# Retention and a soft mixture of experts on one core: input and weight loads of 8 KB per partition, and a separate ring of eight small tiles

## The chip, the cores and the metric

The kernel runs on one core of a Trainium2 chip. The metric is the device time of one execution in microseconds (us). The kernel before takes 169.75 us (median of three runs, 169.55 to 169.78).

## The reference

The reference computes a decayed linear attention (a "retention") over 4 sequences of 768 tokens with 8 heads of 64, and sends its output through a soft mixture of 8 experts with 4 slots each. Cut to what matters:

```python
state = np.zeros((B, H, D, D))                       # B 4, H 8, S 768, D 64
for t in range(S):
    state = gamma * state + einsum('bhd,bhe->bhde', k[:, :, t], v[:, :, t])
    y[:, :, t] = einsum('bhd,bhde->bhe', q[:, :, t], state) / sqrt(D)
x = y as [3072 tokens, 512]
logits = x @ phi                                     # [3072, 32 slots]
d = softmax(logits, over the tokens)                 # dispatch
slot_in = d.T @ x                                    # [32, 512], 4 slots for each expert
for e in range(8):
    slot_out[e] = relu(slot_in[e] @ w1[e]) @ w2[e]   # 512 -> 1024 -> 512
out = softmax(logits, over the slots) @ slot_out     # combine
```

All of it is float32. The inputs are 58 MB, of which q, k and v take 24 MB (the key is read in two layouts) and w1 and w2 16.8 MB each; the output is 6.3 MB.

## The kernel before

**Steps.** The tokens are cut into 24 chunks of 128 (4 sequences of 6 chunks), and the main loop at L359 has one step for each chunk. A step i has these parts on TensorE: `scores(i)` (k times q, L182), `attend(i)` (the carried state times q, L202, and v times the masked scores, L207), `state(i)` (L226) and `natural(i)` (four transposes, L234). The loop issues them shifted by one: attend(i), state(i), scores(i+1), natural(i). VectorE masks the scores (L187) into a tile called A and scales the output of attend into the tile x (L213). GpSimd scales v in place (L169) as soon as v has landed. ScalarE copies the state (L228) and the transposed x (L235). Each four steps make a group with some more work: logits (L245), a running softmax over the tokens, dispatch (L278, L287) and the weights for combine (L303 to L313).

**Behind the steps.** The last group is finished (L397 to L434), `hidden(g, k)` multiplies the slots by w1 (L445) for two halves g of the experts and four blocks k of the model dimension, `hidden_t` transposes the hidden layer into two tiles hT (L459, L463), and the loop at L531 multiplies by w2 (L537) in three blocks of 256, 128 and 128 output columns. `finish` takes a block that is complete: it copies it (L500), sums it over the experts with one matmul (L504), writes it as a tile s4 (L506, L507), and multiplies it with the combine weights c4T (L519). The result is copied out of PSUM by VectorE (first half of a tile, L525) and by ScalarE (second half, L522) into a tile `ot`, which one DMA writes out (L523). The outputs of one block are spread between the w2 matmuls of the next. There are 12 such tiles of 512 KB.

**What orders the work.** TensorE's instructions are in the order of the code; a scheduler orders the other engines. SyncE (SP) issues every DMA, in order, on one queue. The framework gives each DMA the next of eight semaphores, and a DMA is issued only once the one eight places before it has landed; so at most eight are on their way. A tile pool gives a buffer to a new tile as soon as the last reader of an old one is done, and the writer of the new tile (a DMA, or an engine) waits for that.

**Buffers.** One pool, `ring`, has 48 tiles of 4 KB per partition (512 KB). Everything large lives there: the inputs of a step in two tiles (kq with k and q transposed, loaded at L154, vk with v and k, L163 to L168), the w1 and w2 tiles (L139, L143), A and x, the combine weights (c4s, c4T), the hidden layer and hT, s4 and `ot`. Inputs are issued two steps ahead in the code (L365, L369), and weight tiles are dealt between them: 34 over the steps (NPRE, L361), then a few at a time (TAIL, HLOAD). The queue runs ahead of the steps as far as the eight semaphores and free buffers let it.

Of the kernel before, what the change touches and what calls it, by code (L numbers as in the profile page):

```python
# [77 lines left out]
def retention_soft_moe_kernel(  # L78
    ctx: ExitStack,
    tc: tile.TileContext,  # L80
    kq_in: bass.AP,
    vk_in: bass.AP,
# [12 lines left out]
    ps = ctx.enter_context(tc.tile_pool(name="ps", bufs=1, space=PSUM))  # L95

# [27 lines left out]
    weights = [("w1", 4 * g + j, k) for g in range(2) for k in range(NK) for j in range(4)]  # L124
    for cb, (_, w) in enumerate(BLOCKS):
        for g in range(2):
            if w == 64:
                weights += [("w2", 4 * g + 2 * j, cb) for j in range(2)]
            else:
                weights += [("w2", 4 * g + j, cb) for _ in range(NFC // FPS[w]) for j in range(4)]  # L130

    def load_weights(n):
        for _ in range(n):
            if not weights:
                return
            which, e, k = weights.pop(0)
            t = slot()
            if which == "w1":
                nc.sync.dma_start(t, w1[e, k * 128:(k + 1) * 128, :])  # L139
                w1t[e, k] = t  # L140
            else:
                n = 1024 if BLOCKS[k][1] == 64 else FPS[BLOCKS[k][1]] * BLOCKS[k][1]
                nc.sync.dma_start(t[:, 0:n], w2[w2n[0]:w2n[0] + 128 * n].rearrange("(p n) -> p n", n=n))  # L143
                w2n[0] += 128 * n
                if BLOCKS[k][1] == 64:
                    w2t[e, k], w2t[e + 1, k] = [t[:, 0:512]], [t[:, 512:1024]]
                else:
                    w2t.setdefault((e, k), []).append(t)
# [3 lines left out]
    def load_kq(i):  # L152
        t = slot()
        nc.sync.dma_start(t, kq_in[i])  # L154
        st[i] = dict(kT=t[:, 0:512].rearrange("p (g t) -> p g t", t=C),
                     qT=t[:, 512:1024].rearrange("p (g t) -> p g t", t=C))

    def load_vk(i):
        t = slot()
        v = t[:, 0:512].rearrange("p (h e) -> p h e", e=D)  # L160
        st[i].update(v=v, kn=t[:, 512:1024].rearrange("p (h e) -> p h e", e=D))
        if i % NC == NC - 1:
            nc.sync.dma_start(t[:, 0:512], vk_in[i, :, 0:512])  # L163
        elif i == 0:
            nc.sync.dma_start(t[:, 0:512], vk_in[i, :, 0:512])
# [434 lines left out]
```

## Time and profile before

| | |
|---|---|
| time, median of three runs | 169.75 us |
| span of the profiled execution (its own time, first to last instruction) | 168.4 us |
| TensorE (PE) busy | 153.6 us, 91% |
| VectorE (DVE), ScalarE (ACT), GpSimd (POOL) busy | 93.6, 42.0, 30.5 us |
| queue of the kernel's DMAs (q1) | 18,432 packets, 64.26 MB, busy 97.4% of the span |
| loads of 512 KB, median from issue to landing | 10.1 us |
| the 12 output DMAs of 512 KB, median from issue to landing | 4.3 us |

Time that lies outside the span is the 1.35 us between 168.4 and the median. A line such as "L187 DVE" names a line of the kernel and the engine. PE is TensorE, PEld its weight loads, SPq the queue of SyncE that issues the DMAs. In the view of waits, a row has the waiting engine and line, who ended the wait, the total in us, how often, and the longest. In the chain of waits (the work that ended last, followed back), a row has the start, the length and what it was. A matmul of two float32 operands appears as two records ("x16" for eight matmuls). The granted TensorE clock is 0.997 of full speed over the span.

### The profile page before, as it was taken

The page shows a single profiled execution, that of the slowest core. Times are in us where ns is not written, and L with a number is a line of the kernel's source. Part 1 is how long each engine was busy: PE and PEld are TensorE (multiplying, and loading weights), DVE is VectorE, ACT ScalarE, POOL GpSimd, SP SyncE. Part 2 cuts the span into 40 slices and gives each one's busy share as a digit, 9 for nine tenths or more (in the row PEclk, how much of TensorE's full clock was granted, in tenths as well). Part 3 has the DMA queues.
Part 4 walks back from the last instruction along what each step waited for, and adds up shares of the span by engine and source line. Part 5 has one row for each costly group of instructions (what it writes and reads, how often), then busy time and mean ns, then how long its engine had stood idle before and what let it go on. Part 6 is the DMA issues. An engine that isn't in the chain of part 4 may idle for free.

```text
span 168.4 us, 5648 instructions
## 1 busy us (share of the span) xinstructions
PE 153.6 (91%) x2370; PEld 109.6 (65%) x2370; DVE 93.6 (56%) x299; ACT 42.0 (25%) x104; POOL 30.5 (18%) x40
## 2 busy tenths in 40 slices
PE   8699779999999999999989799999999999999940
PEld 2577667687868786888678578867432546666620
DVE  0576445596677876694777566984223121355550
ACT  3022213232423141323212232315202030043330
POOL 0252222230304122232223221300050000000000
PEclk9999999999999999999999999999999999999998
DMA  6999999999999999999999999999999999969966
GB/s 185 324 416 411 408 402 415 401 410 406 410 407 406 407 409 406 408 409 404 407 407 411 405 409 406 403 384 367 378 312 404 415 412 406 412 263 397 384 266 263
DMA packets 18458, 64.62 MB, mean 384 GB/s; under 512 B 2048, under 2 KB 2432, under 8 KB 18432
## 3 DMA queue, kind: packets, MB, share of 16 engines
q1 hardware_dynamic: 18432, 64.26, 97.4%
q8 instruction: 19, 0.31, 0.8%
q14 instruction: 7, 0.06, 0.1%
HBM read 57.96 MB, written 6.29 MB: 381 GB/s over the span
## 4 chain that ended last, share of the span: by engine, by line
PE 50%; DMA 40%; DVE 3%; SPq 2%; issue 1%; DVEq 0%
DMA r<-in_kq_dram 18%; DMA r<-in_w_dram 18%; PE sc L537 9%; PE sc L182 6%; PE y L445 4%; PE y L207 4%; DMA r<-in_vk_dram 4%; PE xp L234 3%; PE sm L245 3%; PE y L202 3%; PE xp L445 2%; PE S L445 2%; PE sm L287 2%; PE S L226 2%; PE sm L519 2%; PE sm L331 1%
## 5 line engine op out<-in xcount | busy, mean ns | idle before, releaser
L187 DVE TENSOR_TENSOR r<-sc,kt 128x256 f32<-128x256 f32 x94 | 33.3, 417 | 17.1 <-PE sc L182 16.1
L169 POOL TENSOR_TENSOR r<-r,kt 128x512 f32<-128x512 f32 x24 | 25.1, 1044 | 75.5 <-DMA r<-in_vk_dram 51.1
L213 DVE SCALAR_TENSOR_TENSOR r<-y,kt,ysc 128x128 f32<-128x128 f32 x96 | 27.7, 343 | 9.6 <-PE y L207 6.7
L182 PE MATMUL sc<-r 64*128 64x128 f32 x376 | 27.4, 284 | 4.4 <-DMA r<-in_kq_dram 4.1
L207 PE MATMUL y<-r 128*64 128x128 f32 x384 | 27.3, 280 | 2.6 <-POOL r L169 2.4
L182 PEld LDWEIGHTS sc<-r 64*128 64x128 f32 x376 | 23.1, 187 | 7.3 <-issue 4.0
L207 PEld LDWEIGHTS y<-r 128*64 128x64 f32 x384 | 21.3, 136 | 7.3 <-POOL r L169 3.8
L235 ACT COPY r<-xp 128x512 f32<-128x512 f32 x23 | 13.5, 586 | 42.9 <-PE xp L234 33.3
L234 PE MATMUL xp<-kt,r 128*128 128x128 f32 x96 | 16.5, 287 | 0.1
L537 PE MATMUL sc<-r 128*32 128x128 f32 (+1 forms) x384 | 15.9, 310 | 0.0
L234 PEld LDWEIGHTS xp<-kt,r 128*128 128x128 f32 x96 | 10.6, 141 | 7.0 <-DVE r L187 3.4
L537 PEld LDWEIGHTS sc<-r 128*32 128x32 f32 x384 | 10.6, 110 | 6.0 <-issue 2.9
L228 ACT COPY sst<-S 128x256 f32<-128x256 f32 x20 | 7.5, 373 | 27.6 <-PE S L226 27.5
L202 PE MATMUL y<-r,sst 64*64 64x128 f32 x320 | 13.3, 282 | 0.0
L226 PE MATMUL S<-r 128*64 128x64 f32 x320 | 13.1, 222 | 0.0
L226 PEld LDWEIGHTS S<-r 128*64 128x64 f32 x320 | 12.3, 138 | 0.0
L202 PEld LDWEIGHTS y<-r,sst 64*64 64x64 f32 x320 | 8.5, 132 | 3.3 <-issue 2.1
L445 PE MATMUL y<-r,siT 128*32 128x512 f32 x64 | 8.2, 597 | 0.0
L245 PE MATMUL sm<-r,phis 128*32 128x128 f32 x192 | 7.3, 276 | 0.0
L245 PEld LDWEIGHTS sm<-r,phis 128*32 128x32 f32 x192 | 5.4, 109 | 1.4 <-issue 1.0
L313 POOL TENSOR_TENSOR cnat<-cnat,cz 128x128 f32<-128x128 f32 x6 | 2.4, 401 | 17.5 <-DVE cz L312 14.5
L287 PE MATMUL sm<-r,p 128*32 128x512 f32 x40 | 5.3, 605 | 0.0
(112 smaller groups left out, 124.2 us busy)
## 6 DMA issues: line engine op xcount, KB each, us to landing
r<-in_w_dram SPq DMA_DIRECT2D x64, 512.0 KB, 10.1
r<-in_kq_dram SPq DMA_DIRECT2D x24, 512.0 KB, 10.1
r<-in_vk_dram SPq DMA_DIRECT2D x19, 512.0 KB, 10.1
out_dram<-r SPq DMA_DIRECT2D x12, 512.0 KB, 4.3
r<-in_vk_dram SPq DMA_DIRECT2D x6, 256.0 KB, 9.6
kt<-in_consts_dram SPq DMA_DIRECT2D x1, 136.0 KB, 3.1
kt<-in_consts_dram SPq DMA_DIRECT2D x1, 78.0 KB, 5.6
phis<-in_phi_dram SPq DMA_DIRECT2D x1, 64.0 KB, 6.2
```

What stands on the lines that cost most here:

```text
L169: nc.gpsimd.tensor_tensor(v, v, vsc[:, i % NC, :].unsqueeze(2).broadcast_to([128, H, D]), ALU.mult)
L182: nc.tensor.matmul(sc[g // 2][r][:, g % 2, :], s["kT"][sl, g, :], s["qT"][sl, g, :], start=True, stop=True)
L187: nc.vector.tensor_tensor(A[:, r, 2 * hf:2 * hf + 2], sc[hf][r], mask.unsqueeze(1).broadcast_to([128, 2, C]), ALU.mult)
L202: nc.tensor.matmul(y[b][o:o + D, gl, :], sst[sl, g, :], s["qT"][sl, g, :], start=(gl == 0), stop=False, skip_group_check=True)
L207: nc.tensor.matmul(y[g // 2][o:o + D, g % 2, :], s["v"][:, 2 * g + r, :], s["A"][:, r, g, :], start=(c == 0 and g % 2 == 0), stop=True, sk ...
L213: nc.vector.scalar_tensor_tensor(yT[:, g, :], y[g // 2][:, g % 2, :], ybs[:, c, g:g + 1], ysc[:, g, :], ALU.mult, ALU.mult)
L226: nc.tensor.matmul(S_[r * D:(r + 1) * D, g, :], s["kn"][:, 2 * g + r, :], s["v"][:, 2 * g + r, :], start=(c == 0 and g == 0), stop=True, s ...
L234: nc.tensor.transpose(xp[:, g * 128:(g + 1) * 128], s["yT"][:, g, :], ident)
L235: (nc.vector.tensor_copy if i == NSTEP - 1 else nc.scalar.copy)(s["xn"], xp)
L245: nc.tensor.matmul(q["ltp"][32 * j:32 * j + 32, :], phis[:, p, :], st[GRP * g + j]["yT"][:, p, :], start=(p == 0), stop=(p == NPAIR - 1), ...
L445: nc.tensor.matmul(hp[g][half][32 * j:32 * j + 32, :], siT[:, k, :], w1t[4 * g + j, k][:, half * 512:(half + 1) * 512], start=(k == 0), st ...
L537: nc.tensor.matmul(op[32 * j:32 * j + 32, :w], hT[fc // 4][:, fc % 4, 4 * g + j, :], t[:, f * w:(f + 1) * w], start=(g == 0 and fc == 0), ...
```

## The change

The ring is split in two pools. `big` has 20 tiles of 8 KB per partition (1 MB), for inputs and weights alone; `ring` keeps 8 tiles of 4 KB for all the rest. Together they take the 192 KB per partition that the 48 tiles took. A step's k, q, v and k are one array now and land in one tile with one DMA (`load_in`), where there were two; for the first step the pieces stay apart, and each sixth step leaves out the last quarter, as before. A w1 tile holds two experts, and a w2 tile all of one expert's 256 columns or two experts' 128 columns. So 32 weight loads of 1 MB stand where 64 of 512 KB were. NPRE goes from 34 tiles to 15, TAIL from (2, 2, 1, 2) to (1, 1, 1, 1), and behind that two tiles are asked for at a time where four were. The host lays the arrays out to match. What TensorE computes, and in which order, stays the same. The diff, cut to its core:

```diff
-TAIL = (2, 2, 1, 2)
-HLOAD = 4
+TAIL = (1, 1, 1, 1)
-NPRE = 34
+NPRE = 15
-NRING = 48
-FPS = {256: 4, 192: 4, 128: 8, 64: 8}
+NRING = 8
+NBIG = 20
...
+    big = ctx.enter_context(tc.tile_pool(name="big", bufs=NBIG))
+
+    def large():
+        return big.tile([128, 2048], F32, name="b", tag="b")
...
-    weights = [("w1", 4 * g + j, k) for g in range(2) for k in range(NK) for j in range(4)]
+    weights = [("w1", 4 * g + 2 * jj, k) for g in range(2) for k in range(NK) for jj in range(2)]
     for cb, (_, w) in enumerate(BLOCKS):
...
+        weights += [("w2", e, cb) for e in range(0, NE, 256 // w)]
...
-            t = slot()
+            t = large()
             if which == "w1":
-                nc.sync.dma_start(t, w1[e, k * 128:(k + 1) * 128, :])
-                w1t[e, k] = t
+                nc.sync.dma_start(t, w1[e // 2, k])
+                w1t[e, k], w1t[e + 1, k] = t[:, 0:FF], t[:, FF:2 * FF]
...
+                nc.sync.dma_start(t, w2[w2n[0]])
+                w2n[0] += 1
+                w = BLOCKS[k][1]
+                for j in range(256 // w):
+                    w2t[e + j, k] = t[:, j * NFC * w:(j + 1) * NFC * w]
...
-    def load_kq(i):
-        t = slot()
-        nc.sync.dma_start(t, kq_in[i])
+    def load_in(i):
+        t = large()
+        if i == 0:
+            nc.sync.dma_start(t[:, 0:1024], in_[i, :, 0:1024])
+            nc.sync.dma_start(kt[:, 0:K_FIRST], consts[:, 0:K_FIRST])
+            nc.sync.dma_start(t[:, 1024:1536], in_[i, :, 1024:1536])
+            nc.sync.dma_start(t[:, 1536:2048], in_[i, :, 1536:2048])
+        elif i % NC == NC - 1:
+            nc.sync.dma_start(t[:, 0:1536], in_[i, :, 0:1536])
+        else:
+            nc.sync.dma_start(t, in_[i])
...
+    def scale_v(i):
+        v = st[i]["v"]
         nc.gpsimd.tensor_tensor(v, v, vsc[:, i % NC, :].unsqueeze(2).broadcast_to([128, H, D]), ALU.mult)
...
         if i + 2 < NSTEP:
-            load_kq(i + 2)
+            load_in(i + 2)
         state(i)
         if i + 2 < NSTEP:
-            load_vk(i + 2)
+            scale_v(i + 2)
...
     for k in range(NK):
         hidden(0, k)
-        load_weights(HLOAD if k == 0 else 4)
+        load_weights(2)
```

Where instructions move, the order on the engines shows it. TensorE's order is the same in both. SP's order changes from its fifth DMA on, behind the first step's inputs. Before (r_86, r_137 and r_198 are the k and q of steps 1, 2 and 3, r_89, r_149 and r_209 their v and k; the last number is the columns, 1024 of them are 512 KB):

```order
L154 DMA r_86<-in_kq_dram 128x1024
L346 DMA kt_66<-in_consts_dram 128x156
L168 DMA r_89<-in_vk_dram 128x1024
L348 DMA phis_69<-in_phi_dram 128x128
L139 DMA r_120<-in_w1_dram 128x1024
L154 DMA r_137<-in_kq_dram 128x1024
L168 DMA r_149<-in_vk_dram 128x1024
L139 DMA r_173<-in_w1_dram 128x1024
L154 DMA r_198<-in_kq_dram 128x1024
L168 DMA r_209<-in_vk_dram 128x1024
L139 DMA r_233<-in_w1_dram 128x1024
L139 DMA r_235<-in_w1_dram 128x1024
```

And in the changed kernel (b_88, b_135, b_194 and b_250 are the inputs of steps 1 to 4):

```order
L159 DMA b_88<-in_x_dram 128x2048
L343 DMA kt_69<-in_consts_dram 128x156
L345 DMA phis_72<-in_phi_dram 128x128
L159 DMA b_135<-in_x_dram 128x2048
L138 DMA b_169<-in_w1_dram 128x2048
L159 DMA b_194<-in_x_dram 128x2048
L159 DMA b_250<-in_x_dram 128x2048
L138 DMA b_283<-in_w1_dram 128x2048
```

The v and k of a step now lands with its k and q; the first weight tile of 512 KB stood ahead of step 2's inputs and now a tile of 1 MB stands behind them; step 4's inputs come right behind step 3's, where two weight tiles lay between.

On VectorE, in the output stage, the copies into `ot` of the first block (L525 before, L522 now; sm, y, S and xp are the PSUM tiles they read), the copy of the second block's sum (os, from sc1) and its s4 (the CAST) stand so before, with the semaphores that each waits for (DMAHW0 to 7 are the eight of the DMAs):

```order
L525 COPY r_2139<-sm_2140 128x512 [waits PE_49]
L525 COPY r_2147<-y1_2148 128x512 [waits PE_49]
L525 COPY r_2167<-S_2168 128x512 [waits DMAHW6_49,PE_49]
L525 COPY r_2187<-xp_2188 128x512 [waits PE_49]
L525 COPY r_2195<-sm_2196 128x512 [waits PE_49]
L500 COPY os_2207<-sc1_2102 128x128 [waits PE_49]
L525 COPY r_2214<-sm_2215 128x512 [waits DMAHW2_49,PE_49]
L506 CAST r_2208<-y0_2231 128x128 [waits DMAHW5_49,PE_49]
```

And in the changed kernel:

```order
L522 COPY r_2031<-sm_2032 128x512 [waits PE_49]
L522 COPY r_2039<-y1_2040 128x512 [waits PE_49,Activation_49]
L497 COPY os_2099<-sc1_1994 128x128 [waits PE_49]
L522 COPY r_2059<-S_2060 128x512 [waits DMAHW5_49,DVE_49,Activation_49]
L522 COPY r_2079<-xp_2080 128x512 [waits DMAHW6_49,DVE_49,Activation_49]
L522 COPY r_2087<-sm_2088 128x512 [waits PE_49]
L522 COPY r_2106<-sm_2107 128x512 [waits DMAHW7_49,DVE_49,Activation_49]
L503 CAST r_2100<-y0_2123 128x128 [waits DVE_49,DMAHW0_49,PE_49,Activation_49]
```

The copy of os moved ahead of the third `ot`. In the changed kernel the outputs use the semaphores 5, 6, 7, 0, 1, 2 and so on in turn, so the third `ot` (r_2059) waits for the landing of the first output, the fourth (r_2079) for the second, the sixth (r_2106) for the third, and the s4 of the second block (r_2100) for the fourth. The DMA waits of the rows before are on weight tiles, whose buffers these tiles take over.

On ScalarE, where the last group is dispatched, the rows before are (S and y are transposes of combine weights, p the dispatch weights, ysc the last group's sum):

```order
L431 COPY lts<-sm 128x128
L280 COPY p<-sm 128x128
L408 ACTIVATE wj<-nmc,nms 128x2
L295 COPY ysc<-y_1805 128x128 x4
L334 CAST r<-S 128x512
L334 CAST r<-y_1795 128x512
```

And in the changed kernel:

```order
L428 COPY lts<-sm 128x128
L332 CAST r<-S 128x512
L278 COPY p<-sm 128x128
L405 ACTIVATE wj<-nmc,nms 128x2
L332 CAST r<-y_1707 128x512
L293 COPY ysc<-y_1717 128x128 x4
```

The two casts of combine weights moved ahead of the copies p and ysc, for which TensorE waits.

More of the change, by code (lines that the diff above doesn't have):

```diff
@@ L80, in retention_soft_moe_kernel @@
     tc: tile.TileContext,
-    kq_in: bass.AP,
-    vk_in: bass.AP,
+    in_: bass.AP,
     phi: bass.AP,
@@ L123, in retention_soft_moe_kernel @@
     w1t, w2t, w2n = {}, {}, [0]
-    weights = [("w1", 4 * g + j, k) for g in range(2) for k in range(NK) for j in range(4)]
+    weights = [("w1", 4 * g + 2 * jj, k) for g in range(2) for k in range(NK) for jj in range(2)]
     for cb, (_, w) in enumerate(BLOCKS):
[L126 to L130, printed above, removed]
+        weights += [("w2", e, cb) for e in range(0, NE, 256 // w)]
     def load_weights(n):
@@ new lines, in load_weights @@
+                w1t[e, k], w1t[e + 1, k] = t[:, 0:FF], t[:, FF:2 * FF]
+            else:
+                nc.sync.dma_start(t, w2[w2n[0]])
[3 more added lines that the diff above has]
+                    w2t[e + j, k] = t[:, j * NFC * w:(j + 1) * NFC * w]
+    st = {}
+    def load_in(i):
[9 more added lines that the diff above has]
+            nc.sync.dma_start(t, in_[i])
+        v = t[:, 1024:1536].rearrange("p (h e) -> p h e", e=D)
+        st[i] = dict(kT=t[:, 0:512].rearrange("p (g t) -> p g t", t=C),
+                     qT=t[:, 512:1024].rearrange("p (g t) -> p g t", t=C), v=v,
+                     kn=t[:, 1536:2048].rearrange("p (h e) -> p h e", e=D))
@@ L335, in copy_c @@
                        c4p[q, half].rearrange("p j t -> p (j t)"))
-    load_kq(0)
-    nc.sync.dma_start(kt[:, 0:K_FIRST], consts[:, 0:K_FIRST])
+    load_in(0)
     nc.vector.tensor_tensor(ysc.rearrange("p g (a b) -> p g a b", b=8),
@@ L343, in retention_soft_moe_kernel @@
                             .broadcast_to([128, NPAIR, 16, 8]), ALU.mult)
-    load_vk(0)
-    load_kq(1)
+    scale_v(0)
+    load_in(1)
     nc.sync.dma_start(kt[:, K_FIRST:], consts[:, K_FIRST:])
-    load_vk(1)
+    scale_v(1)
     nc.sync.dma_start(phis, phi)
@@ L478, in retention_soft_moe_kernel @@
     copy_c(1, 1)
-    load_weights(4)
+    load_weights(2)
     hidden(1, 1)
     hidden_t(0)
-    load_weights(4)
+    load_weights(2)
     hidden(1, 2)
@@ L486, in retention_soft_moe_kernel @@
         copy_c(2, half)
-    load_weights(4)
+    load_weights(2)
     hidden(1, 3)
@@ L568, in lay_out @@
     phi = np.asarray(moe_phi).reshape(H, D, NSLOT)[heads].reshape(NPAIR, 128, NSLOT).transpose(1, 0, 2)
-    w1 = np.asarray(moe_w1).reshape(NE, H, D, FF)[:, heads].reshape(NE, DM, FF)
+    w1 = np.asarray(moe_w1).reshape(NE, H, D, FF)[:, heads].reshape(NE // 2, 2, NK, 128, FF).transpose(0, 2, 3, 1, 4)
     w2 = []
     for c0, w in BLOCKS:
-        x = np.asarray(moe_w2)[:, :, c0:c0 + w]
-        if w == 64:
-            x = x.reshape(NE // 2, 2, NFC, 128, w).transpose(0, 3, 1, 2, 4)
-        else:
-            x = x.reshape(2, 4, NFC // FPS[w], FPS[w], 128, w).transpose(0, 2, 1, 4, 3, 5)
-        w2.append(x.reshape(-1))
-    w2 = np.concatenate(w2)
-    return dict(kq=np.concatenate([tr(k), tr(q)], axis=2), vk=np.concatenate([nat(v), nat(k)], axis=2), phi=phi, w1=w1, w2=w2, consts=constants())
+        x = np.asarray(moe_w2)[:, :, c0:c0 + w].reshape(NE * w // 256, 256 // w, NFC, 128, w)
+        w2.append(x.transpose(0, 3, 1, 2, 4).reshape(-1, 128, 2 * FF))
+    return dict(x=np.concatenate([tr(k), tr(q), nat(v), nat(k)], axis=2), phi=phi,
+                w1=w1.reshape(NE // 2, NK, 128, 2 * FF), w2=np.concatenate(w2), consts=constants())
 _OUT = (DM, NTOK)
```

23 lines of the change are left out of this document (2 added, 21 removed).

## The prediction

> **What bounds the kernel now.** I read the page first, for the span and for how full the DMA queue is.
>
> ```profile
> span 168.4 us, 5648 instructions
> DMA  6999999999999999999999999999999999969966
> GB/s 185 324 416 411 408 402 415 401 410 406 410 407 406 407 409 406 408 409 404 407 407 411 405 409 406 403 384 367 378 312 404 415 412 406 412 263 397 384 266 263
> r<-in_w_dram SPq DMA_DIRECT2D x64, 512.0 KB, 10.1
> ```
>
> The queue runs at 401 to 416 GB/s from 8 to 109 us (slices of 4.2 us), dips, and goes on until the outputs. A load lands 10.1 us after its issue because eight are always on their way. So the queue looks like the bound; the chain of waits, in order of time, says for how long it is.
>
> ```profile
> 83.91 10.12 DMA r<-in_kq_dram
> 94.03 0.14 issue
> 94.16 1.16 PE sc L182 x16
> ...
> 114.34 0.44 PE S L331 x4
> ...
> 119.32 1.00 PE xp L445 x8
> 120.31 0.86 PE y L445 x8
> ...
> 159.26 0.30 DVE os L500
> ```
>
> The last load that the end follows from lands at 94.03. From there to 159.26 the chain is TensorE, but for a few us on VectorE. So before 94 us TensorE waits for inputs now and then, and behind it nothing in the queue is late. How much the waits are, TensorE's view of them tells, from 7.5 to 26 us and from 26 to 112 us:
>
> ```profile
> PE sc L182 <- DMA r<-in_kq_dram: 2.4, 2, 1.2
> PE y L207 <- POOL r L169: 0.3, 1, 0.3
> ```
> ```profile
> PE sc L182 <- DMA r<-in_kq_dram: 1.7, 3, 1.1
> PE y L207 <- POOL r L169: 0.5, 1, 0.5
> ```
>
> That is 4.9 us in all; POOL's L169 waits for v in turn. This is what earlier inputs can win.
>
> **Part 1, the loads of the steps.** What 1 MB costs, the issue queue shows: each issue waits for a landing eight places before, so issues keep the landings' distance.
>
> ```profile
> 52.02 0.33 SPq L154 DMA_DIRECT2D r<-in_kq_dram  x1
> 53.31 0.33 SPq L168 DMA_DIRECT2D r<-in_vk_dram  x1
> 53.97 1.61 SPq L139 DMA_DIRECT2D r<-in_w_dram  x2
> ```
>
> The second issue follows a landing of 512 KB (1.29 us), the third one of 256 KB, a sixth step's v alone (0.66). Twice 0.66 is 0.03 more than 1.29, so 0.03 is fixed for each DMA, and 1 MB takes 2 x 1.29 - 0.03 = 2.55. Bounds: 2.58 (nothing saved) and 2.53 (the rows' last digits). The Trainium skill, page "DMA: Bandwidth & Descriptors", section "Rules for kernel authors", asks for at least 1 MiB in a DMA for full bandwidth, and its section "Bandwidth" has 425 GB/s for 16 MB (and 341 for 1 MB): by 425 a load of 1 MB would take 2.47 us (an estimate), and the sum below would be 0.9 lower. The trace is against most of it: 512 KB already run at 401 to 416 GB/s, since eight overlap.
>
> When an input lands is counted in KB ahead of it, its own included. Step 1's k and q end at 1,672 KB before and 2,184 now; step 3's at 4,886 and 5,398; step 4's at 6,934 and 6,422; step 8's at 13,846 and 13,334; step 20's at 34,838 and 33,302. 512 KB are 1.29 us. Steps 1 and 3 get theirs 1.3 later, all from the fourth on earlier, up to 3.9 us at step 20, because 28 tiles of weights stood ahead there and now 24 stand.
>
> ```profile
> 8.62 1.16 PE L182 MATMUL sc<-r 64*128 64x128 f32 x16
> ...
> 11.27 1.09 PE L207 MATMUL y<-r 128*64 128x128 f32 x16 [0.29 <-POOL r L169]
> ...
> 12.90 1.16 PE L182 MATMUL sc<-r 64*128 64x128 f32 x16
> ...
> 17.89 1.16 PE L182 MATMUL sc<-r 64*128 64x128 f32 x16 [1.12 <-DMA r<-in_kq_dram]
> ...
> 23.02 1.16 PE L182 MATMUL sc<-r 64*128 64x128 f32 x16 [1.25 <-DMA r<-in_kq_dram]
> ```
>
> These are the scores of steps 1, 2, 3 and 4 on TensorE, and v times scores of step 1. A step without a wait takes 17.89 - 12.90 - 1.12 = 3.87. Step 1: 8.62 + 1.3 = 9.9, of which the wait of 0.29 for v takes a part, so step 2 starts at 12.90 + 1.0 = 13.9. Step 3 would be ready at 17.8, its input lands at 17.89 + 1.3 - 0.1 = 19.1 (0.1 for what the larger DMAs save up to there). Step 4 can start at 19.1 + 3.87 = 22.97; its input is there at 21.7. Before it started at 23.02: the first four steps come out even. Of the later waits, 1.7 for k and q and 0.5 for v, all go, as every input comes 0.6 us or more earlier. Sum of the steps: **-2.2**. Late next is TensorE itself, with 15.74 busy of 16 us where nothing waits:
>
> ```profile
> 94.00:110.00 16.00, 15.74 (x266) 12.42 (x266) 11.35 (x37) 4.15 (x12) 4.58 (x5) 1.00 1.03 407
> ```
>
> Bounds: -1.0 (0.7 more lost at the start, the 0.5 for v stays) and -3.0 (0.8 more, by the rival on the inputs). The scaling of v on POOL now sits ahead of the copies of rep there, whose reader comes at 114 us: no cost.
>
> **Part 2, ScalarE's order at the last group.** A cast now stands ahead of the copy p, for which the dispatch matmuls (L287) wait.
>
> ```profile
> L334 ACT CAST r<-S x1: 628/628/628, 117.3 to 117.3; 128x512 fp32r<-128x512 f32 x1
> 115.10 0.27 ACT L280 COPY p<-sm 128x128 f32<-128x128 f32 x1 [0.37 <-PE sm L278]
> ```
>
> It can start when the transposes S end (114.34 + 0.44 = 114.78) and ends at 115.41, 0.3 behind 115.10: **+0.3**, between 0 and 0.6. The other moves on POOL and VectorE before the output stage lie under TensorE.
>
> **Part 3, when the weights are in.** The 20 large tiles hold 16 tiles of w1 and four of w2 when the steps are over; the fifth w2 tile needs the first w1 tile back. That is read last by the second expert in the second half of hidden(0, 0): 119.32 + 1.00 + half of 0.86 = 120.75, with -2.2 + 0.3 = -1.9 at 118.85. The four tiles ahead are asked for by the end of the last step (at the latest 114.34 - 1.9 = 112.4) and are in by 117 even if two of them are still to come (2 x 2.55), so the queue is empty. What 512 KB take from issue to landing in an empty queue is the least of the outputs:
>
> ```profile
> DMA to landing us min/median/max: 2.9/4.3/6.0
> ```
>
> 1 MB takes 2.9 + 1.3 = 4.2, so the fifth lands at 123.05. Later w1 tiles come free two in 1.86 us, faster than 2 x 2.55, so eleven more follow at 2.55: the last lands at 151.1. Before, the last load was issued at 139.5 and loads of that line took 8.8 in the median and 11.2 at most, so it landed at 148.3 to 150.7:
>
> ```profile
> L143 SPq DMA_DIRECT2D r<-in_w_dram x32: 327/328/1449, 99.2 to 139.5; - x32
> DMA to landing us min/median/max: 4.9/8.8/11.2
> ```
>
> So the loads end no earlier although TensorE is 1.9 ahead. The w2 matmuls need the last tile only at about 155 and don't wait.
>
> **Part 4, two tiles for the outputs.** Of the eight small tiles three hold c4T and two hT until the last w2 matmul, and one s4. Two are left for `ot`, where before dozens were. The third output's copies wait until the first output has landed, the fourth's for the second, and the second block's s4 for the fourth. Behind a waiting copy VectorE holds every later copy; TensorE holds the w2 matmuls, which stand in its order behind output matmuls that need the copied PSUM. The rows of before:
>
> ```profile
> 148.52 0.35 SPq L523 DMA_DIRECT2D out_dram<-r  x1
> 149.97 0.34 SPq L523 DMA_DIRECT2D out_dram<-r  x1
> 149.60 0.69 DVE L525 COPY r<-S 128x512 f32<-128x512 f32 x1 [0.63 <-PE S L519]
> ...
> 152.05 0.43 PE S L519
> 152.48 0.23 PE sm L519
> 152.72 0.23 PE xp L519
> ...
> 153.98 0.29 DVE L506 CAST r<-y 128x128 fp32r<-128x128 f32 x1 [0.53 <-PE y L504]
> 154.30 0.29 DVE L507 TENSOR_TENSOR r<-y,r 64x128 fp32r<-64x128 f32 x1
> ...
> 155.17 0.43 PE y L519
> ```
>
> The first output is issued at 148.52 - 1.9 = 146.6, but on the one queue it lies behind the loads: it lands at 151.1 + 1.3 = 152.4, the second at 153.7. The copy of S (0.69) then ends at 153.1 and the matmul of 152.05 starts at 153.2, where 150.15 would have been its time: 3.05 of waiting. The copy of xp ends at 153.7 + 0.7 = 154.4; the matmul of 152.72 needs it and starts at 154.45 instead of 153.2 + 0.67 = 153.85: 0.6. With this copy the fourth output is issued at 154.45 and lands 2.9 later, at 157.35. s4 takes 153.98 to 154.6 in the rows, 0.6, and is done at 157.95. The matmul of 155.17, which reads it, could start at 155.17 + 1.73 (the lag so far: 154.45 - 152.72) = 156.9 and starts at 158.05: 1.15. Behind it the waits (fifth and sixth outputs) end before they are asked for. Sum: **+4.8**.
>
> **The sum.** 168.4 - 2.2 + 0.3 + 4.8 = 171.3 of span; with the 1.35 between span and median (169.75 - 168.4), 172.65, told as **172.6 us**.
>
> **The rivals.**
>
> *The two tiles are enough (faster).* If outputs landed before their tile is asked for, part 4 were nothing: 168.4 - 2.2 + 0.3 + 1.35 = 167.85. It is decided at the first output: it must land by 147.7 (149.60 - 1.9), 1.1 after its issue. The least landing time of 2.9 speaks against it. Chance 0.08.
>
> *The inputs were worth more (faster, a little).* The view of waits gives weight loads of TensorE, waiting for VectorE behind late scores, and these may be late inputs too:
>
> ```profile
> PEld xp L234 <- DVE r L187: 3.4, 4, 0.8
> ```
>
> With 3.4 more the sum is 172.65 - 3.4 = 169.25. Against it: the scaled scores follow TensorE's own scores in steps that waited for nothing. Chance 0.07.
>
> *The outputs don't stand behind the loads (no change).* If the first lands 2.9 after its issue, at 149.5, the waits fall to 0.1 at S, 0.8 at xp (the second output at 149.97 - 1.9 + 2.9 = 150.95) and 1.15 at s4 (the fourth at 151.7 + 2.9): 2.05 in place of 4.8, and 169.9. For it: nothing quoted shows an output that overtakes or doesn't. Against it: it is one queue, and loads land in order, 1.29 apart. Chance 0.10.
>
> *TensorE's clock falls in the wait (slower still).* The window behind the last matmul shows the granted clock at 0.91:
>
> ```profile
> 162.30:168.40 6.10, 0.34 (x1) 0.04 (x1) 0.99 (x2) 0.97 (x2) 0.00 (x0) 0.91 0.66 265
> ```
>
> 0.09 of 6.1 us at half speed are 1.1 us, so about 4.8 us of idling were enough; the wait of 3.05 is shorter, but its upper bound (below) isn't. The matmuls from 152.05 to 155.17 would take 3.1 more, of which the next two waits (0.6 and 1.15) hide 1.75: 172.65 + 1.35 = 174.0. The Trainium skill, page "TensorE: Matmul & The Clock Gate", section "Part 1: The HAM clock gate (the "warmup" mystery)", says that one idle window of about 3.4 us drops the clock to half; no run here shows so short a one. Chance 0.10.
>
> *The rows of 8 KB are moved as 4 KB (the change doesn't do what it says).* Then 1 MB is 2.58, and the twelve loads end 0.35 later (12 x 0.03): 173.0. Chance 0.05.
>
> **How the numbers follow.** The forecast keeps 0.60. Its own bounds: the steps 0.8 less or 1.2 more, part 2 0.3 either way, the wait for s4 up to 1.4 longer (an output at its median, 4.3), twelve loads at 2.53 or 2.58 0.3 either way: 171.2 when all the gains come together, 174.8 when the two largest losses and half of the rest do. To hold eight in ten the range takes in the no-change rival, the clock and part of the small gain: 169.5 to 174.8. Faster by over 0.2% (0.34 us, about what a measurement of this kernel can tell) is 0.08 + 0.07 and 0.03 of the no-change rival, 0.18; within it 0.06; slower 0.76.
>
> **What would show it.** Right: no wait of TensorE for inputs behind step 4; the last load near 151; a copy of VectorE from S in the output stage that waits for an output DMA, and TensorE idle for some 3 us at about 150 to 153, then twice about 1; fewer and larger packets. Wrong: TensorE through the output stage without idling (first rival), or a first output that lands well before the last load (third); waits for kq or weights in the steps (part 1), or for w2 (part 3).

## The result, and the profile after

The changed kernel takes 175.93 us (median of 4 runs, 175.42 to 177.54); the kernel before, on the same chip, 169.67 (169.55 to 169.78). The ratio is 1.038, interval 1.034 to 1.043: slower, as forecast, but by 6.3 us where 2.9 were forecast, and outside the range of 169.5 to 174.8. The profiled execution took 176.38 with a span of 174.6; the forecast had 171.3 of span. Times here and below are medians of a kernel's fast executions, and the slow ones (one of 248.2 us among them) are left out.

From the page of the changed kernel, the span, TensorE, its clock and the DMA queue in 40 slices of 4.4 us:

```profile
span 174.6 us, 5506 instructions
PE   8769899999999999999999999999999998087840
PEclk9999999999999999999999999999999999957998
DMA  5999999999999999999999999709999999666575
GB/s 143 340 417 419 420 420 421 417 426 411 416 421 419 419 417 416 423 413 415 424 417 416 420 418 411 325 32 347 424 430 420 417 420 394 274 249 243 203 299 226
```

Three holes are new. TensorE has one at slice 34, counted from 0 (148 to 153 us), its clock is down in the two slices behind it, and the DMA queue stands nearly still at slice 26 (32 GB/s, 113.5 to 118 us). From slice 5 on TensorE has no gap before the holes: it was to be 1.9 us ahead when the weight stage begins, and it is 4.15 ahead (the first matmul behind the last dispatch starts at 112.28 where it was at 116.43).

Most of the lead (3.73 us of it) comes from the steps. These two rows of the windows view hold the same 1,307 matmuls, from the scores of step 5 up to those of step 23, of before and of after (length, TensorE busy, weight loads, VectorE, ScalarE, POOL, clock, DMA share, GB/s):

```profile
28.05:107.84 79.79, 77.18 (x1307) 61.40 (x1306) 55.88 (x186) 22.15 (x60) 19.68 (x22) 1.00 1.03 407
```
```profile
28.05:104.11 76.06, 76.06 (x1307) 61.18 (x1306) 54.95 (x186) 22.19 (x60) 20.69 (x23) 1.00 1.01 418
```

Before, 2.61 of 79.79 us were idle; after, none of 76.06. The other 1.12 us were inside matmuls that had longer records, and no row of waits showed those. The queue moves 418 GB/s now, 407 before.

What became of the lead shows in TensorE's view of waits of the changed kernel (waiting line, who ended it, us in total, times, longest):

```profile
PE S L516 <- DVE r L522: 5.6, 1, 5.6
PE sc L180 <- DMA b<-in_x_dram: 2.2, 2, 1.7
PE y L516 <- DVE r L504: 1.3, 1, 1.3
PE y L205 <- POOL b L167: 1.1, 1, 1.1
```

S waits for a copy into the third `ot`, y for s4 of the second block. The second and fourth row are the first steps. The chain of waits of the changed kernel shows what stands behind the first and third row:

```profile
145.25 0.59 ACT r L519
145.85 0.02 issue
145.86 7.98 DMA out_dram<-r
153.84 0.03 issue
...
153.96 0.70 DVE r L522
154.66 0.02 SPq L520
154.69 0.03 issue
154.72 5.19 DMA out_dram<-r
159.90 0.03 issue
...
160.03 0.30 DVE r L503
160.33 0.02 issue
160.35 0.30 DVE r L504
160.66 0.14 issue
160.79 0.47 PE y L516
```

The second output goes out at 145.86 and lands at 153.84, behind the last weight load (landed at 151.37). The fourth `ot` waits for it (the copy at 153.96), and s4 of the second block waits for the fourth output, which lands only 5.19 us after its issue. From 145 to 161 us the end hangs on two output DMAs. These stretches of the changed kernel, columns as above, show the queue and the clock:

```profile
114.00:121.00 7.00, 7.00 (x64) 2.68 (x67) 2.63 (x8) 0.90 (x2) 0.40 (x1) 1.00 0.44 157
121.00:148.00 27.00, 26.90 (x375) 14.12 (x367) 5.65 (x24) 4.00 (x7) 0.00 (x0) 1.00 1.01 419
148.00:152.80 4.80, 0.00 (x0) 0.00 (x0) 0.33 (x2) 0.09 (x1) 0.00 (x0) 1.00 0.72 273
152.90:159.70 6.80, 6.05 (x61) 3.68 (x61) 2.60 (x4) 2.15 (x4) 0.00 (x0) 0.50 0.69 276
159.80:168.00 8.20, 6.00 (x86) 4.15 (x86) 4.37 (x10) 2.30 (x5) 0.00 (x0) 1.00 0.55 219
```

From 114 to 121 us the queue has little to do, since the next load waits for a free large tile. TensorE idles through all of the 4.8 us from 148 us (5.6 us in all, by the row of waits), and then works at half clock for 6.8.

Forecast and profile, step by step (us):

| | forecast | profile |
|---|---|---|
| TensorE ahead of before at the first matmul behind the last dispatch | 1.9 | 4.15 |
| last weight load lands | 151.1 | 151.37 |
| first and second output land | 152.4, 153.7 | 152.61, 153.84 |
| matmul of S, matmul of xp | 153.2, 154.45 | 153.48, 154.71 |
| fourth output: issue to landing | 2.9 | 5.19 |
| matmul that reads s4 of the second block | 158.05 | 160.79 |
| span | 171.3 | 174.6 |

### The profile page after: what moved, and what is told of

The parts are those of the page before. It is cut to its first block, busy times and chain, and to the rows that moved or that the text cites. A ratio compares the mean times of both kernels' runs of the same rounds, so it can differ in the third digit from the quotient of the medians.

```text
span 174.6 us, 5506 instructions
## 1 busy us (share of the span) xinstructions
PE 156.1 (89%) x2370; PEld 111.3 (64%) x2370; DVE 92.2 (53%) x299; ACT 42.3 (24%) x104; POOL 30.6 (18%) x40
## 4 chain that ended last, share of the span: by engine, by line
PE 75%; DMA 15%; SPq 3%; DVE 2%; issue 1%; ACT 1%; DVEq 0%; ACTq 0%
PE sc L180 13%; PE y L205 13%; DMA out_dram<-r 8%; DMA b<-in_x_dram 7%; PE xp L232 7%; PE sc L534 7%; PE y L200 6%; PE S L224 5%; PE y L442 4%; PE sm L243 4%; PE sm L285 3%; PE xp L442 2%; PE S L442 2%; PE sm L329 1%; PE sm L516 1%
## 5 line engine op out<-in xcount | busy, mean ns | idle before, releaser
L167 POOL TENSOR_TENSOR b<-b,kt 128x512 f32<-128x512 f32 x24 | 25.0, 1042 | 69.2 <-DMA b<-in_x_dram 54.5
L180 PE MATMUL sc<-b 64*128 64x128 f32 x376 | 27.9, 288 | 2.2 <-DMA b<-in_x_dram 2.2
L205 PE MATMUL y<-r,b 128*64 128x128 f32 x384 | 27.1, 279 | 1.1 <-POOL b L167 1.1
L180 PEld LDWEIGHTS sc<-b 64*128 64x128 f32 x376 | 23.4, 190 | 5.2 <-issue 2.3
L205 PEld LDWEIGHTS y<-r,b 128*64 128x64 f32 x384 | 21.3, 136 | 5.4 <-issue 3.8
L534 PE MATMUL sc<-b,r 128*32 128x128 f32 (+1 forms) x384 | 17.4, 331 | 0.0
L534 PEld LDWEIGHTS sc<-b,r 128*32 128x32 f32 x384 | 11.6, 118 | 6.3 <-issue 3.6
L200 PE MATMUL y<-b,sst 64*64 64x128 f32 x320 | 13.3, 282 | 0.0
L224 PE MATMUL S<-b 128*64 128x64 f32 x320 | 13.1, 222 | 0.0
L224 PEld LDWEIGHTS S<-b 128*64 128x64 f32 x320 | 12.3, 138 | 0.0
```

The source lines that it names most:

```text
L167: nc.gpsimd.tensor_tensor(v, v, vsc[:, i % NC, :].unsqueeze(2).broadcast_to([128, H, D]), ALU.mult)
L180: nc.tensor.matmul(sc[g // 2][r][:, g % 2, :], s["kT"][sl, g, :], s["qT"][sl, g, :], start=True, stop=True)
L200: nc.tensor.matmul(y[b][o:o + D, gl, :], sst[sl, g, :], s["qT"][sl, g, :], start=(gl == 0), stop=False, skip_group_check=True)
L205: nc.tensor.matmul(y[g // 2][o:o + D, g % 2, :], s["v"][:, 2 * g + r, :], s["A"][:, r, g, :], start=(c == 0 and g % 2 == 0), stop=True, sk ...
L224: nc.tensor.matmul(S_[r * D:(r + 1) * D, g, :], s["kn"][:, 2 * g + r, :], s["v"][:, 2 * g + r, :], start=(c == 0 and g == 0), stop=True, s ...
L534: nc.tensor.matmul(op[32 * j:32 * j + 32, :w], hT[fc // 4][:, fc % 4, 4 * g + j, :], t[:, fc * w:(fc + 1) * w], start=(g == 0 and fc == 0) ...
```

## The experiments

Theory: the two small tiles for the outputs cost the time, and the miss lies at the fourth output. Rivals: the large loads themselves, the missing tiles, the clock.

### Do the outputs' tiles cost the time?

**Outputs in large tiles**, whose first owners are done by then:

```diff
-                ot = slot()
+                ot = large()[:, 0:1024]
```

> The changed kernel with one edit: the twelve output tiles come from the pool of large tiles, whose w1 tiles are free by then, so that no output waits for another output. Theory (the two small tiles cost the time, and behind that wait the DMA queue is next): no copy of the output stage waits for an output DMA, TensorE keeps its 4 us of lead at the dispatch of the last group (112.3 where it was 116.4 in the kernel before), the last load lands near 151, twelve outputs of 1.25 us follow it, the span is about 167.5 and the time 169.2 us (168.4 to 170). Rival 1 (TensorE is the bound once the waits are gone): the 4 us of lead reach the end, span 164.3, time 165.7. Rival 2 (the large loads themselves slow the end): 173 us or more.

Measured: 169.59 us, ratio to before 1.0005 (0.998 to 1.003); the profiled execution took 170.9, with a span of 169.1. The theory holds: no copy waits for an output, and 6.3 us are back. But the lead (2.8 us here) brings nothing either, because the queue is the bound: it rests between 114 and 121 us, the last load lands at 152.73, and twelve outputs follow at 1.25 us each, up to 167.71.

```profile
114.00:121.00 7.00, 7.00 (x63) 3.60 (x66) 2.08 (x9) 1.45 (x6) 1.05 (x2) 1.00 0.20 66
121.00:150.00 29.00, 29.00 (x390) 14.99 (x382) 8.99 (x30) 5.36 (x10) 0.00 (x0) 1.00 1.01 417
```

**The waits in the kernel before**: three tiles of their own for s4 and the outputs.

```diff
-NRING = 48
+NRING = 45
+    fin = ctx.enter_context(tc.tile_pool(name="fin", bufs=3))
-        s4 = slot()
+        s4 = fin.tile([128, 1024], F32, name="f", tag="f")
-                ot = slot()
+                ot = fin.tile([128, 1024], F32, name="f", tag="f")
```

> The kernel before with one edit: s4 and the outputs share a pool of three tiles of 4 KB, the other 45 stay with the rest, and loads stay at 512 KB. This gives the copies of the output stage the same waits as in the changed kernel (third output for the first, fourth for the second, s4 of the second block for the fourth). Theory (these waits alone cost the time): from the landings of before, S waits 0.65, xp 0.6 more, s4 of the second block some 2.3 more: span 171.9, time 173.3 us (172.0 to 174.6). Rival (the cost comes with the 1 MB loads, which keep the first outputs behind them): 169.7 to 170.5 us.

**Its control**: 45 tiles, with outputs and s4 in the one pool.

```diff
-NRING = 48
+NRING = 45
```

> The kernel before with one edit: 45 tiles in its pool for 48, with outputs and s4 in the same pool as before. It is the control for the run in which s4 and the outputs had three tiles of their own: whether the weight loads that stood still there between 112 and 124 us did so for the three missing tiles or for the outputs' waits (which come 30 us later). Theory (the three tiles matter little by themselves): the last load lands 1 to 1.5 later than before (152 for 150.45), twelve outputs follow at 1.25: span 168.7, time 170.1 us (169.6 to 171). Then most of the 8.5 us of the run with the pool of three are the waits. Rival (the missing tiles are most of it): 174 us or more.

Measured: 177.9 us with the pool of three (ratio 1.049, 1.046 to 1.053) and 171.7 with 45 tiles (1.012, 1.010 to 1.014). Both were forecast too low. Three tiles fewer cost 2 us, since the last load lands at 153.07 where it was 150.44; the waits cost 6.2 on top of that, with loads of 512 KB. So they don't need the large loads. TensorE's waits in the run with the pool of three have the two rows of the changed kernel:

```profile
PE S L520 <- DVE f L526: 2.8, 1, 2.8
PE y L520 <- DVE f L508: 1.5, 1, 1.5
```

### Order or size of the loads?

**The order alone**, in the kernel before:

```diff
-NPRE = 34
+NPRE = 29
```

> The kernel before with one edit: NPRE 29 for 34, which puts about as many KB of weights ahead of the late steps' inputs as in the changed kernel (24 tiles of 512 KB ahead of step 20 where 28 stood), with loads of 512 KB as before. Theory (the order of the loads is what makes the inputs early): the waits of TensorE for kq and v behind 26 us vanish and the last group's dispatch comes 2 to 3.5 us earlier than in the kernel before; the end gains less, since the last load still lands near 150.5 and twelve outputs follow: 169.0 us (168.2 to 169.8). Rival (the size of the loads is what does it, 2.48 us for 1 MB where two of 512 KB take 2.57): TensorE's lead is 1 us or less.

**Fewer still**:

```diff
-NPRE = 34
+NPRE = 24
```

> The kernel before with NPRE 24 for 34, five tiles of weights fewer over the steps than in the run with 29. Theory (with 29 TensorE's waits for inputs behind the third step are gone already, and the queue never rests from 8 us to the end): no further gain, 166.8 us within 0.5. Rival (the inputs were still late at places): 165.8 us or less. Rival (the weights now come too late for the first hidden matmuls): TensorE waits for w1 and 168 us or more.

Measured: 166.79 us (0.983, 0.981 to 0.986) and 166.69 (0.982, 0.981 to 0.984). The order alone gives TensorE 5.0 us at the first matmul behind the last dispatch (111.41), more than the changed kernel's 4.15, with loads of 512 KB. And here the lead pays, by 2 us more than was forecast: from 112 to 121 us the queue moves 406 GB/s where it moved 372 (the rows below, before and with 29), the last load lands at 149.13 where it was 150.44, and the outputs are ready behind it and land every 1.24 us, the last at 164.03 where it was 167.59. With 24 nothing more is won, as forecast.

```profile
112.00:121.00 9.00, 9.00 (x95) 5.93 (x89) 3.65 (x14) 3.42 (x12) 0.00 (x0) 1.00 0.98 372
112.00:121.00 9.00, 9.00 (x82) 4.07 (x85) 4.08 (x9) 2.28 (x7) 2.18 (x3) 1.00 1.02 406
```

**The size alone**: the changed kernel with each load as two of 512 KB.

```diff
-                nc.sync.dma_start(t, w1[e // 2, k])
+                for h in range(2):
+                    nc.sync.dma_start(t[:, 1024 * h:1024 * h + 1024], w1[e // 2, k, :, 1024 * h:1024 * h + 1024])
...
-            nc.sync.dma_start(t, in_[i])
+            nc.sync.dma_start(t[:, 0:1024], in_[i, :, 0:1024])
+            nc.sync.dma_start(t[:, 1024:2048], in_[i, :, 1024:2048])
```

> The changed kernel with one edit: each load of 1 MB is issued as two of 512 KB into the halves of its tile (k and q, then v and k), so tiles, order and pools stay and only the size of the DMAs goes back. Theory (order and the two small tiles decide, size is worth 0.09 us for each MB): k and q land 1.3 before v, so the first steps start earlier; the late inputs are still early enough, so the lead at the last dispatch stays at 3 us or more; twelve loads behind the first free w1 tile end 1 us later, and with them the outputs: 176.9 us (175.5 to 178). Rival (the size of the DMAs makes the lead): the lead falls to 2 us or less. Rival (the large DMAs make the outputs land late): 173 us or less.

Measured: 177.26 us (1.046, 1.042 to 1.051). The lead stays (scores of step 23 at 104.06, changed kernel 104.11), the last load lands at 153.12 where it was 151.37, the wait of S is 6.9 and that of y 0.6. Size is worth some 1.3 us by the medians (the intervals overlap by a little, at 1.042 to 1.043), and none of it is the lead.

**Large inputs beside small weights**, in the kernel before; `load_in` is that of the changed kernel, with tiles from the new pool, and the first eight weight tiles behind the steps are halves of such tiles:

```diff
-NPRE = 34
+NPRE = 29
-NRING = 48
+NRING = 40
+NIN = 4
...
+    inp = ctx.enter_context(tc.tile_pool(name="inp", bufs=NIN))
```

> The kernel before with NPRE 29 and the inputs of a step in one DMA of 1 MB, in a pool of four tiles of 8 KB of their own; the ring keeps 40 tiles of 4 KB, and the first eight weight tiles behind the steps go into the halves of the four input tiles. So the larger DMAs cost the outputs no tiles. Theory (with the order alone the DMA queue is the bound to the end, at 1.28 us for 512 KB, and 1 MB takes 0.08 less): 23 loads of it save 1.8 us of queue, of which TensorE's last outputs leave 1.5: 165.2 us (164.6 to 166.5) where NPRE 29 alone gave 166.8. Rival (four input tiles let the queue run too little ahead, or the first steps wait for 1 MB): 167 us or more.

Measured: 167.8 us (0.990, 0.987 to 0.992), worse than the order alone, as the rival had it. Which of the rival's two reasons it is wasn't tried.

**Large loads with the outputs out of the way**: 21 large and 6 small tiles, outputs in large tiles, inputs of steps 1 to 3 in halves.

```diff
-NRING = 8
-NBIG = 20
+NRING = 6
+NBIG = 21
...
+        elif i < 4:
+            nc.sync.dma_start(t[:, 0:1024], in_[i, :, 0:1024])
+            nc.sync.dma_start(t[:, 1024:2048], in_[i, :, 1024:2048])
```

> The run with outputs in large tiles, with two edits: 21 large tiles and 6 small ones, so that one weight load more is in before the first w1 tile comes free, and the inputs of steps 1 to 3 in two halves (k and q ahead of v and k). What the large loads are worth where the outputs wait for nothing. Theory (the queue stands still from 114 to 121 us for want of tiles, and the end is what the queue still has to move): one tile more ends the loads 2.5 us earlier and the earlier first steps 0.5 to 1: 166.5 us (165.8 to 167.5). Rival (six small tiles are too few where the last group needs c4s and x at once): TensorE waits there and 169 us or more.

Measured: 166.28 us (0.981, 0.979 to 0.983), as the theory had it: faster than both kernels. The queue rests less from 114 to 121 us:

```profile
114.00:121.00 7.00, 7.00 (x65) 2.18 (x67) 2.60 (x8) 0.90 (x2) 0.40 (x1) 1.00 0.73 284
```

Whether it is faster than the small loads in the better order, the intervals don't tell (0.979 to 0.983 and 0.981 to 0.984).

### Why the outputs land late

**Outputs on a queue of their own**:

```diff
-                        nc.sync.dma_start(out[c0 + m * 128:c0 + m * 128 + mw, q * 1024:(q + 1) * 1024], ot[0:mw])
+                        nc.scalar.dma_start(out[c0 + m * 128:c0 + m * 128 + mw, q * 1024:(q + 1) * 1024], ot[0:mw])
```

> The changed kernel with one edit: ScalarE issues the output DMAs, so they have a queue of their own and don't stand behind SyncE's weight loads; the tiles stay as they are. Theory (in the changed kernel the first outputs are late because they lie behind the loads in one queue, and the copies that wait for their tiles hold TensorE): the first output lands 4 to 5 us after its issue, near 149 where it was 152.6; TensorE's wait at S falls from 5.6 to 1 or 2; the loads share the engines with the outputs and end later, near 155; 171 to 173.5 us. Rival (the outputs land late for another reason, the engines being full): first landing at 151 or later and 175 us or more.

Measured: 178.62 us (1.054, 1.050 to 1.058). The rival was right by landing and time. The first output, issued at 144.05 on ScalarE's own queue, sends its first packet at 147.53 and lands at 151.98; on the loads' queue it took 144.37 to 152.61. Until 147.53 the 16 engines moved the loads' packets alone, and from then to 151 us packets of both queues side by side. So the forecast's cause (behind the loads in one queue) was too narrow, though its times held: a queue of its own brings the output no engines of its own. Why its first packet waits 3.5 us all the same isn't shown. By the Trainium skill, page "DMA: Bandwidth & Descriptors", section "Issuing engines are not separate DMA queues", DMAs of all issuers run interleaved on the same 16 engines; the trace agrees from 147.53 us on. ScalarE also held the second output back until 152.16, behind a copy that waited for the first, so the 178.62 us are not the price of the second queue alone.

The other five runs are about the fourth output. Its landing is 16 events, one from each engine: in the changed kernel fifteen came by 157.40 and one at 159.90. The DMA view of 156.5 to 159.5 us names what is in between:

```profile
q1 hardware_dynamic: 247, 0.88, 73.4%
q8 instruction: 1, 0.02, 2.0%
```

One packet of 16,384 bytes on the queue of instructions, from 156.87 to 157.81: the kernel's own code. By the times of the packets, one engine's eight of the output came behind it, the last one ending at 159.43. Such packets go out about every 250 recorded instructions of TensorE, 19 in this execution as in that of before. So their place can be moved from the other end of the program.

**140 instructions more at the start**, in the changed kernel:

```diff
-WARM = 5
-WN = 256
+WARM = 40
+WN = 32
```

> The changed kernel with one edit: the five warm-up matmuls of 256 columns at the start become forty of 32, which take about as long but put 140 instructions more ahead of everything else on TensorE. In the traces so far a packet of 16,384 bytes on the queue named instruction goes out about every 256 instructions of TensorE, and the one at 156.87 us in the changed kernel (4,567 instructions of TensorE in) holds one of the 16 DMA engines while the fourth output is on its way: that engine ends 2.5 us behind the others, and s4 of the second block waits for it. With 140 more in front, that packet goes out at about 144.4 and the next near 160. Theory (it makes the fourth output late): the fourth output lands some 3 us after its issue where it took 5.2, and the time falls by 2.0 to 2.5: 173.6 us (173.0 to 174.6). Rival (the fourth output is late for what is queued on the engines): 175.9 us as before, and one engine still lags.

**Zeros in the wait, to keep the clock up**: three matmuls ahead of the second S.

```diff
+                    if n_co[0] == 10:
+                        fill = ps.tile([128, 512], F32, name="y0")
+                        for _ in range(3):
+                            nc.tensor.matmul(fill[0:1], nc.const_aps.tensor(0.0, [128, 1], F32),
+                                             nc.const_aps.tensor(0.0, [128, 512], F32), start=True, stop=True)
```

> The changed kernel with one edit: three matmuls on zeros (512 columns, some 5 us in all, result unused) stand on TensorE where it waits for the copy of S, so that it isn't idle and its clock should stay at full speed (it was granted 0.50 from 153 to 159 us). Theory (the half clock and the late fourth output lie side by side, each hiding the other): the clock stays at 1.00, but the matmul that reads s4 of the second block still starts near 160.8, since s4 waits for the fourth output: 175.7 us (175.0 to 176.5). Rival (the half clock is what costs the time behind the wait): that matmul starts near 158.5 and the time is 173.6 us or less.

**Both edits**:

> Both edits together: the forty short warm-up matmuls, which moved the instruction packet out of the fourth output's way (it landed 2.7 us after its issue, but the matmul behind it still started at 160.36, at half clock), and the three matmuls on zeros in the wait. Theory (two causes side by side, either of which is enough): with both gone s4 is ready at about 158.9 and the matmul that reads it starts near 159.1 where it was 160.8: 174.2 us (173.5 to 174.9). Rival (something else sets that matmul): 175.5 us or more, as with either edit alone.

**Six matmuls for three**, and **six with the short warm-ups**:

```diff
-                        for _ in range(3):
+                        for _ in range(6):
```

> The run with the wait filled, mended: three matmuls on zeros took 2.75 us where 5 were meant, 3.2 us of idling were left, and the clock fell all the same. Now six of them, 5.5 us, which leave about 0.5 us of idling. Theory (half clock and late fourth output side by side): the clock stays at 1.00 from 147 to 160 us; the matmul that reads s4 of the second block still waits for the fourth output where that is late (issue to landing of 4 us or more), and starts 0.9 us behind its landing: 174.5 to 176 us. Rival (the half clock alone is the cost): that matmul starts within 3.5 us of the third output's matmul and the time is 173.6 us or less.

> Six matmuls on zeros and the forty short warm-ups together: neither the half clock nor the instruction packet on the fourth output's way. Theory (the two causes side by side, and nothing else): from the matmul of S to the matmul that reads s4 of the second block it takes about 4.8 us (1.25 to the matmul of xp, 3.6 to the landing of the fourth output and its s4) where it took 7.3 in the changed kernel and 6.0 with either one gone: 174.2 us (173.5 to 174.9). Rival (something else sets that matmul): 6 us or more between the two, and 175.3 us or more.

The first column is the median time, the others are from the one profiled execution of each kernel (us; "clock" is the granted clock from the matmul of S to the one that reads s4):

| run | us | clock | fourth output, issue to landing | S to the matmul that reads s4 |
|---|---|---|---|---|
| changed kernel | 175.93 | 0.50 | 5.19 | 153.48 to 160.79: 7.31 |
| three zeros | 176.53 | 0.50 | 4.22 | 153.08 to 159.43: 6.35 |
| six zeros | 177.09 | 1.00, from 159.6 on 0.50 | 4.15 | 153.66 to 159.94: 6.28 |
| short warm-ups | 175.68 | 0.50 | 2.70 | 154.30 to 160.36: 6.06 |
| both, three zeros | 175.51 | 0.50 | 2.69 | 153.64 to 159.63: 5.99 |
| both, six zeros | 175.33 | 1.00 | 2.74 | 153.57 to 158.44: 4.87 |
| forecast | 172.6 | 1.00 | 2.9 | 153.2 to 158.05: 4.85 |

The three zeros took 2.75 us in place of 5 and didn't keep the clock. The other runs separate the causes: with the packet moved the output lands in 2.7 us, but TensorE at half clock then sets the matmul; with the clock kept, the late output sets it; with both gone it is 4.87, where the forecast had 4.85 (in part by luck: the landing took 2.74 for 2.9, and from there to the matmul it was 0.89 for 0.70). Two chains show it, with the packet moved and the clock at half, and then with both mended:

```profile
155.53 0.79 PE xp L516
156.32 1.01 PE sc L534 x16
157.34 0.73 PE y L501 x2
158.06 2.29 PE sc L534 x40
160.36 0.53 PE y L516
```
```profile
154.80 0.50 PE xp L521
155.30 0.57 PE sc L539 x16
155.88 0.42 PE y L501 x2
156.30 1.27 PE sc L539 x40
...
157.67 0.30 DVE r L503
...
158.00 0.30 DVE r L504
158.30 0.14 issue
158.44 0.47 PE y L521
```

The forty matmuls took 2.29 us and then 1.27, and s4 is the last to come only in the second.

By their times all five missed the forecasts: 175.68 us where 173.6 was forecast, 176.53 where 175.7 (at most 176.5), 175.51 where 174.2, 177.09 where 174.5 to 176, and 175.33 where 174.2. Each interval overlaps that of the changed kernel. So the two causes are shown at the matmul that reads s4, and not in the time.

With both edits the time as a whole fell far less than that matmul moved: 175.33 (1.031, 1.026 to 1.036) against 1.038 (1.034 to 1.043), 0.6 us in the medians and 1.3 in the spans, where 1.7 were forecast. Of the 2.4 us gained at that matmul 1.1 went behind it: the packet of code, moved to 158.46, now held the fifth output (4.6 us from issue to landing), and a copy waited for that. With six zeros alone the clock fell in the next wait instead (0.50 from 159.6 to 163.0). In these runs mending one late output left the next on the path to the end.

## Why the prediction was wrong, and where it was right

**The step that failed** is in part 4, the price of s4: "With this copy the fourth output is issued at 154.45 and lands 2.9 later, at 157.35." It was issued at 154.72 and landed 5.19 later. The 2.9 was the least landing time of an output in the kernel before; the bound allowed 1.4 more, its median, and 6.0 was in the same row. One DMA engine that loaded code made it late, and the half clock alone would have held the matmul behind it nearly as long: from S to that matmul it took 6.28 us with the late output alone, 6.06 with the half clock alone and 4.87 with neither. That this is within 0.02 us of the forecast is in part luck, since two errors of 0.2 cancel in it. Of the 3.3 us missed in the span 0.28 were there at S, 2.46 came from S to this matmul, and the other 0.56 lie behind it, at the end of the program. The upper end of the range was also added wrongly: 172.6 with the two largest losses (1.4 and 1.2) and half of the rest (0.3) is 175.5, not 174.8, and the 175.93 lie outside that as well.

**The clock rival came true beside the forecast**, not in its place: given a chance of 0.10, because the wait was put at 3.05 us and 4.8 thought enough. The wait was 5.6, since TensorE had more lead; but in one run 2.0 us were enough. By itself it would have cost 1.2 (6.06 against 4.87), close to the 1.35 of the rival.

**Part 1, the steps: right in kind, too small, and worth nothing.** The first four steps came out even (step 4 at 23.01, forecast 22.97). Behind them 3.7 us were won, not 2.2: the sum took only rows that name a DMA or v as releaser, where 2.61 us were idle and 1.12 lay in longer matmuls. The rival that the inputs are worth more was right in kind, with 1.5 us more than the 2.2 where it had 3.4 more, but the lead went into the wait of S. Its cause is the order of the weights, as forecast; the size of the loads gives none of it.

**1 MB was priced at 2.55 us and took 2.48** (landings 2.47 to 2.49 apart from 123.14 to 147.98). By the 425 GB/s in the Trainium skill, page "DMA: Bandwidth & Descriptors", section "Bandwidth", it would be 2.47 (an estimate), which the forecast set aside; the trace is on the skill's side. "Eight overlap" was no argument: in the steps the queue moved 418 GB/s with 1 MB and 407 with 512 KB.

**Part 2** was put at 0.3. From the scores of step 23 to the matmul behind the last dispatch it took 8.17 us, before 8.59; with `NPRE = 29` and ScalarE's order as before 8.11. So the moved casts cost some 0.06.

**Part 3 was right by two errors.** The fifth w2 load was issued at 117.05, not 118.85, but landed at 123.14, 6.1 later and not 4.2. Fifteen of its 16 events came by 121.78, and a packet of code held an engine from 120.94 to 121.87: by these times the same event as at the fourth output. The ten behind it took 2.48 each, 0.07 less than priced, and the last, which shared the engines with the first outputs, 3.39. That loads wait for tiles was seen; that the queue then rests (44% busy from 114 to 121 us, 3.9 us lost) and becomes the bound of the rest was not. So the rival in which two tiles are enough (167.85) was priced too low: with the waits gone the kernel took 169.59, with the queue as its bound.

**The first statement, that behind 94 us nothing in the queue is late, was half of it.** TensorE did set the end before, but the queue was close behind: with 5.0 us of lead (`NPRE = 29`) the kernel gained 2.8.

## What to carry to other kernels

When a ring is split, count what the smaller part must hold at its fullest moment, and price a tile that waits for a DMA to land at that DMA's worst landing, not its best: it has to wait for the slowest of 16 engines. Time won ahead of a wait for DMAs is lost in it; look for what the queue still has to move behind that point before giving a lead any worth. Try the cheap half of a change alone: here the order of the loads, one number, gave 2.8 us, while the change as a whole needed the outputs moved, one large tile more and the first inputs in halves to give 3.4.

## What was new of the hardware

- Code loads share the DMA engines. Packets of 16,384 bytes, one for about 250 recorded TensorE instructions, took 0.9 to 1.4 us on one engine, and an output behind one landed 2.5 us late. By the Trainium skill, page "Runtime: NRT & Kernel Launch", section "Instruction fetch mechanics", code comes in blocks of 16 KiB, 256 instructions, and the cost is mostly hidden; the trace agrees on the size, but hidden it was not.
- The 16 engines drift apart: the load that landed at 94.64 us in the changed kernel was done on its first engine at 89.43. A landing waits for the last of them. What sets them apart over the steps isn't shown.
- The clock changes by windows. In views of 1 us (columns as above) the run with short warm-ups falls at about 150.3 us and comes back at 160.5:

```profile
150.00:151.00 1.00, 0.00 (x0) 0.00 (x0) 0.00 (x0) 0.00 (x0) 0.00 (x0) 0.64 1.01 418
151.00:152.00 1.00, 0.00 (x0) 0.00 (x0) 0.00 (x0) 0.00 (x0) 0.00 (x0) 0.50 0.47 193
...
160.00:161.00 1.00, 1.00 (x11) 0.59 (x3) 0.02 (x1) 0.00 (x0) 0.00 (x0) 0.74 0.61 221
161.00:162.00 1.00, 1.00 (x26) 0.59 (x24) 0.67 (x1) 0.58 (x1) 0.00 (x0) 1.00 0.00 0
```

  That is 10.2 us at half speed; in the changed kernel it was 6.8 (152.9 to 159.7), with six zeros 3.4 (159.6 to 163.0): three, two and one times 3.4. It fell after 5.0 us of idling in the changed kernel, 2.7 with short warm-ups and 2.0 with six zeros, and came back 3.1 to 6.5 us after work began again. By the Trainium skill, page "TensorE: Matmul & The Clock Gate", section "Part 1: The HAM clock gate (the "warmup" mystery)", activity is judged in a free-running window of 3.4 us; the trace agrees on the window, but one that was idle for 2.0 of its 3.4 us was enough, where the page speaks of an idle window. Where the limit lies is open: counted back from the fall in windows of 3.4 us, a window with 1.6 us of idling left the clock up in the changed kernel (146.1 to 149.5), and one with 1.6 dropped it in the run with the pool of three (153.2 to 156.6).
